# Batch 1's expert product in pairs of tiles, and its attention steps issued earlier

## Chip, cores, metric

One core of one Trainium2 chip. The metric is the time of one execution on the device in microseconds (us), median of several runs. TensorE's granted clock (PEclk in the profile, a share of its full speed) is near 1.0 in most runs, and where it is not, the text says so.

## The reference

Linear attention with an RMS norm per head, then layer norm, a two-layer expert with ReLU and a residual. Eight batches of 576 rows, 8 heads of 64.

```python
def _attn_ref(q, k, v, g_norm):          # q, k, v: (8, 8, 576, 64)
    kv = np.einsum('bhsd,bhse->bhde', k, v)
    out = np.einsum('bhsd,bhde->bhse', q, kv)
    rms = np.sqrt(np.mean(out * out, axis=-1, keepdims=True) + 1e-06)
    return out / rms * g_norm

def _moe_ref(x, g_ln, w_ch1, w_ch2):     # x: (8, 576, 512), w_ch1: (512, 2048)
    mu = np.mean(x, axis=-1, keepdims=True)
    var = np.mean((x - mu) ** 2, axis=-1, keepdims=True)
    xn = (x - mu) / np.sqrt(var + 1e-06) * g_ln
    return x + np.maximum(xn @ w_ch1, 0.0) @ w_ch2
```

## The kernel before

The expert's two products for each batch (`mm1`, `mm2`) fill TensorE from front to back. The attention of later batches is woven in between them by an agenda: the products are cut into slots of about 0.87 us, `tick()` starts a slot, and `at(slot, fn)` issues `fn` at its start, in front of that slot's matmuls. A fraction in a slot number only sets an order within the slot.

A batch has four tiles of 128 rows (and a rest). A turn is a transpose. One tile takes this path (shortened):

```python
    def plan_tile(s, make, turn_at, on_pe):
        def first():      # PE: attention product o; ACT: square; DVE: reduction
            t = make(); box.append(t)
            t.o(); t.sq(); t.red()
        def second():     # ACT: root; DVE: reciprocal, y, x, xc
            t = box[0]
            t.y(); t.x(); t.xc()
        def third():      # ACT: variance
            box[0].var()
        def fourth():     # PE: four transposes of xc; ACT: copy to xT_blk
            box[0].turn(on_pe)
        at(s, first); at(s + 2, second); at(s + 6, third); at(turn_at, fourth)
```

`turn` on TensorE uses `ps_m`, a pool of one bank, and `kv_of` (the k-v product of a batch) uses the same bank until ScalarE has cast it. A bank here is one buffer of such a pool. With one in the pool, the next user waits until the one before has been read out:

```python
    ps_m = ctx.enter_context(tc.psum_pool(name="ps_m", bufs=1))
    ps_out = ctx.enter_context(tc.psum_pool(name="ps_out", bufs=2))
# ... (cut)
                tp = ps_m.tile([128, nK, 128], bf16, tag="misc", name="tp")
                for kk in range(nK):
                    nc.tensor.transpose(tp[:, kk, :], self.xc_t[...], identity)
                nc.scalar.copy(dst, tp)
# ... (cut: kv_of)
        kv_ps = ps_m.tile([128, HP, D], f32, tag="misc", name="kv_ps")
        # 40 matmuls into kv_ps
        nc.scalar.copy(kvp[:D, :, :D], kv_ps[:D])
        nc.scalar.copy(kvp[D:, :, D:], kv_ps[D:])
```

Batch 1 turns its q on TensorE (`q_turns`). From batch 2 on, q is copied by VectorE and turned by a transposing DMA:

```python
    def turn_q_dma(b):
        q_p = kv_in.tile([128, JJ, H, D], bf16, tag="qp", bufs=2)
        nc.vector.tensor_copy(q_p.rearrange("p j h d -> p h j d"), q_in[b % NB])
        q_t = qt_pool.tile([128, JJ, HP, 128], bf16, tag="qt", name="qt")
        nc.sync.dma_start_transpose(q_t..., q_p...)
        qts[b] = q_t
```

The agenda that matters here, and the products. Batch 0's second product fills slots 16 to 31, batch 1's first one slots 32 to 47:

```python
    at(21, lambda: kv_of(1))
    q_turns(23, 1)
    for j, s, tn in ((0, 24, 30), (1, 27, 34), (2, 31, 38), (3, 35, 42)):
        plan_tile(s, lambda j=j: main_tile(1, j), tn, True)
    at(46, lambda: rstd_of(1))

    at(36, lambda: kv_of(2))
    at(36.5, lambda: turn_q_dma(2))
    for j, s, tn in ((0, 44, 50), (1, 48, 54), (2, 53, 61), (3, 58, 67)):
        plan_tile(s, lambda j=j: main_tile(2, j), tn, j > 1)
# ... (cut)
    for ts in range(4):
        mm1(1, ts, 1)          # one tile at a time: 128 columns
    mm2(1)
    mm1(2, 0, 2)               # batch 2: pairs, 256 columns
    mm1(2, 2, 2)
```

## Time and profile before

| | before |
|---|---|
| time, median of 3 runs | 291.68 us (291.61 to 291.71) |
| span of the profiled execution | 289.6 us |
| TensorE busy | 281.9 us, 97% |
| granted clock | 1.0 |

The page of the kernel before, its busy line and the shares of the chain of waits by engine (PE is TensorE, PEld its weight loads, DVE VectorE, ACT ScalarE, POOL GpSimd; L402 is line 402 of the kernel):

```profile
PE 281.9 (97%) x2312; PEld 158.6 (55%) x2312; DVE 151.0 (52%) x335; ACT 155.0 (54%) x339; POOL 41.0 (14%) x68
...
PE 93%; DMA 2%; ACT 1%; DVE 1%; POOL 1%; issue 1%; POOLq 0%
```

TensorE is the bound: the chain that ended last runs over it for 93% of the span.

The groups by line and shape, TensorE only, for the expert's first product (columns: line, engine, operation, operands, shape, count, then busy us and the mean ns of one):

```profile
L402 PE MATMUL p<-xT_blk,w_sb 128*128 128x128 bf16 x512 | 31.2, 219 | 0.2
L402 PE MATMUL p<-xT_blk,w_sb 128*128 128x256 bf16 x128 | 14.8, 273 | 0.0
```

The means (219 and 273 ns) are latencies of matmuls that overlap: the starts of the narrow ones are 55.9 ns apart. What one costs is read from starts in the timeline below.

The timeline of TensorE in the kernel before (start us, us, line, operation, operands, shape, count; a group's duration includes the modelled drain of its last matmul, so compare starts):

```profile
42.04 1.03 PE L418 MATMUL p<-w_sb,m 128*128 128x512 bf16 x4
43.13 0.38 PE L170 MATMUL tp<-identity,q_p 128*128 128x128 bf16 x4
...
57.05 0.39 PE L337 MATMUL tp<-identity,xc 128*128 128x128 bf16 x4
57.28 3.74 PE L402 MATMUL p<-xT_blk,w_sb 128*128 128x128 bf16 x64
60.85 0.39 PE L337 MATMUL tp<-identity,xc 128*128 128x128 bf16 x4
...
62.86 0.39 PE L260 MATMUL o_ps<-kv_pack,qt 128*128 128x128 bf16 x4
63.08 3.74 PE L402 MATMUL p<-xT_blk,w_sb 128*128 128x128 bf16 x64
66.66 0.39 PE L260 MATMUL o_ps<-kv_pack,qt 128*128 128x128 bf16 x4
```

Four matmuls of slot 23 start at 42.04 and take 0.86 (216 ns each: 20 of this shape, from 66.88, have the next product behind them at 71.20), so TensorE is free at 42.90; the q turn comes at 43.13, a gap of 0.23. The last three lines are batch 2's first attention product (`o_ps`, 62.86), 64 matmuls of 128 columns, and batch 2's next product: (66.66 - 63.08) / 64 = 55.9 ns each. From 57.05 to 66.66 there is no gap.

The timeline of VectorE in the kernel before, with batch 2's q copy (L201) and tile 3's y and xc:

```profile
56.48 0.82 DVE L201 COPY q_p<-q_in 128x2560 bf16<-128x2560 bf16 x1
...
58.19 0.69 DVE L292 TENSOR_TENSOR y<-o_ps,inv 128x512 f32<-128x512 f32 x1
...
59.84 0.75 DVE L321 SCALAR_TENSOR_TENSOR xc<-x_blk,st_blk,g_ln_sb 128x512 bf16<-128x512 f32 x1
```

The q copy runs ahead of tile 3's steps. It ends at 57.30, and the view of this DMA gives 5.0 us from issue (57.33) to landing, so q lies turned at 62.3. Batch 2's first product wants it at 62.86. There are 0.5 us to spare.

### The profile page before, as it was taken

The numbers are of one execution on the slowest core, as the hardware profiler recorded it, in microseconds if no ns is written. First come the engines' busy times: TensorE is split into PE (matmuls) and PEld (weight loads), VectorE is DVE, ScalarE is ACT, GpSimd is POOL, SyncE is SP. The second block draws the span as 40 slices with busy tenths as digits, with TensorE's granted clock in tenths as the row PEclk, the third lists the DMA queues.
The fourth block names the chain that finished last, engine by engine and source line by source line (L and its number), as shares of the span: only waits on it lengthen the run. The fifth ranks groups of instructions, "written<-read, shape, count | busy, mean of one in ns | idle before, by whom it ended". The sixth has DMA issues, their size and how long they took to land.

```text
span 289.6 us, 5791 instructions
## 1 busy us (share of the span) xinstructions
PE 281.9 (97%) x2312; PEld 158.6 (55%) x2312; DVE 151.0 (52%) x335; ACT 155.0 (54%) x339; POOL 41.0 (14%) x68
## 2 busy tenths in 40 slices
PE   7889999999999999999999999999999999999995
PEld 2579755996569644444444444444444444444444
DVE  5775028847997793765366925762578300220022
ACT  3467755885469832882189418920894076016500
POOL 8522520032032003200410023000000000000000
PEclk9999999999999999999999999999999999999999
DMA  7999999469999918995997179938202510131033
GB/s 215 203 206 203 201 202 218 109 99 188 155 177 160 151 40 158 205 167 102 148 208 103 42 146 194 178 75 164 54 18 53 112 36 0 38 81 28 0 74 73
DMA packets 64378, 36.10 MB, mean 125 GB/s; under 512 B 31836, under 2 KB 59356, under 8 KB 64352
## 3 DMA queue, kind: packets, MB, share of 16 engines
q0 software_dynamic: 28016, 17.76, 44.2%
q1 hardware_dynamic: 35824, 17.25, 30.5%
q10 hardware_dynamic: 512, 0.72, 0.7%
q8 instruction: 18, 0.29, 0.4%
q14 instruction: 8, 0.07, 0.1%
HBM read 36.71 MB, written 9.44 MB: 159 GB/s over the span
## 4 chain that ended last, share of the span: by engine, by line
PE 93%; DMA 2%; ACT 1%; DVE 1%; POOL 1%; issue 1%; POOLq 0%
PE p L418 43%; PE p L402 43%; PE o_ps L260 3%; DMA q_in<-in_q_dram 2%; PE kv_ps L235 2%; PE tp L183 1%; PE p L196 1%; PE tp L337 1%; ACT sq L266 0%; PE tp L170 0%; PE o_half L500 0%; POOL v_in L126 0%; ACT xT_blk L542 0%; ACT m L405 0%; DVE x_blk L278 0%
## 5 line engine op out<-in xcount | busy, mean ns | idle before, releaser
L402 PE MATMUL p<-xT_blk,w_sb 128*128 128x128 bf16 (+2 forms) x1024 | 131.8, 286 | 0.2
L418 PE MATMUL p<-w_sb,m 128*128 128x512 bf16 (+2 forms) x608 | 129.2, 368 | 0.0
L405 ACT ACTIVATE m<-p 128x512 bf16<-128x512 f32 x144 | 85.5, 596 | 43.3 <-PE p L402 41.1
L402 PEld LDWEIGHTS <-w_sb 128*128 128x128 bf16 x1024 | 78.5, 98 | 44.1 <-issue 0.6
L418 PEld LDWEIGHTS <-m 128*128 128x128 bf16 x608 | 56.8, 98 | 61.8
L423 DVE SCALAR_TENSOR_TENSOR o_sb<-p,rstd,x_blk 128x512 f32<-128x512 f32 (+2 forms) x38 | 27.4, 721 | 54.3 <-PE p L418 48.7
L266 ACT ACTIVATE sq<-o_ps 128x512 f32<-128x512 f32 x34 | 20.2, 595 | 41.5 <-PE o_ps L260 41.4
L287 DVE TENSOR_REDUCE ss<-sq 128x8 f32<-128x512 f32 x34 | 23.0, 678 | 11.2 <-ACT sq L266 11.2
L329 ACT ACTIVATE dev<-x_blk,st_blk 128x512 f32<-128x512 f32 x36 | 25.7, 714 | 4.6 <-DVE st_blk L315 4.4
L321 DVE SCALAR_TENSOR_TENSOR xc<-x_blk,st_blk,g_ln_sb 128x512 bf16<-128x512 f32 x34 | 25.6, 752 | 1.2
L292 DVE TENSOR_TENSOR y<-o_ps,inv 128x512 f32<-128x512 f32 x34 | 23.5, 692 | 3.0
L311 DVE SCALAR_TENSOR_TENSOR x_blk<-y,g_norm_sb 128x512 f32<-128x512 f32 x34 | 23.5, 692 | 1.2
L411 DVE RECIPROCAL rstd<-rstd 128x4 f32<-128x4 f32 x9 | 1.6, 174 | 35.3 <-ACT rstd L410 35.3
L304 DVE RECIPROCAL inv<-rms 128x8 f32<-128x8 f32 x36 | 7.2, 201 | 23.0 <-ACT rms L297 23.0
L98 POOL COPY gate<-qt 1x1 bf16<-1x1 bf16 x5 | 0.9, 178 | 114.1 <-DMA qt<-q_p 114.1
L297 ACT ACTIVATE rms<-ss,eps_sb 128x8 f32<-128x8 f32 x36 | 10.7, 297 | 9.5 <-DVE ss L287 8.8
L260 PEld LDWEIGHTS <-qt 128*128 128x128 bf16 (+1 forms) x152 | 9.9, 100 | 7.4 <-issue 1.7
L260 PE MATMUL o_ps<-kv_pack,qt 128*128 128x128 bf16 (+1 forms) x152 | 13.3, 220 | 0.2 <-DVE qt L191 0.2
L196 PE MATMUL p<-fill_sb 128*128 128x512 bf16 x28 | 8.1, 445 | 1.2 <-DVE eps_sb L137 1.2
L329 ACT ACTIVATION_READ_ACCUMULATOR dev<-x_blk,st_blk 128x1 f32 x36 | 6.9, 190 | 0.0
L235 PEld LDWEIGHTS <-k_in 128*64 128x64 bf16 x280 | 5.0, 112 | 2.6 <-issue 2.5
L238 ACT CAST kv_pack<-kv_ps 64x256 bf16<-64x256 f32 x7 | 2.6, 366 | 7.2 <-PE kv_ps L235 7.2
(79 smaller groups left out, 116.8 us busy)
## 6 DMA issues: line engine op xcount, KB each, us to landing
out_dram<-o_sb SPq DMA_DIRECT2D x70, 128.0 KB, 2.4
w_sb<-in_moe_w_ch_dram POOLq DMA_DIRECT2D x8, 512.0 KB, 13.8
k_in<-in_k_dram POOLq DMA_DIRECT2D x7, 320.0 KB, 5.8
v_in<-in_v_dram POOLq DMA_DIRECT2D x7, 320.0 KB, 9.4
q_in<-in_q_dram POOLq DMA_DIRECT2D x7, 320.0 KB, 12.7
q_in<-in_q_dram POOLq DMA_DIRECT2D x8, 256.0 KB, 12.7
k_in<-in_k_dram POOLq DMA_DIRECT2D x7, 256.0 KB, 7.3
v_in<-in_v_dram POOLq DMA_DIRECT2D x7, 256.0 KB, 11.3
```

The source lines that it names most:

```text
L196: nc.tensor.matmul(p1, lhsT=fill_sb[:, :128], rhs=fill_sb, start=True, stop=True)
L260: nc.tensor.matmul(flat[rows, hp * 128:(hp + 1) * 128], lhsT=lhsT_of(hp), rhs=kvp[:, hp, :], start=True, stop=True)
L266: nc.scalar.activation(self.sq_t, self.o_ps, func=AF.Square)
L287: nc.vector.tensor_reduce(self.ss, self.sq_t, axis=AX.X, op=ALU.add)
L292: nc.vector.tensor_mul(self.y_t, self.o_ps, self.inv().to_broadcast([128, H, D]))
L311: nc.vector.scalar_tensor_tensor(x_blk[:, ts].rearrange("p (h d) -> p h d", h=H), in0=self.y_t, scalar=1.0, in1=g_norm_sb.to_broadcast([12 ...
L321: nc.vector.scalar_tensor_tensor(self.xc_t, in0=x_blk[:, self.ts], scalar=st[:, 1, self.ts:self.ts + 1], in1=g_ln_sb, op0=ALU.add, op1=ALU ...
L329: nc.scalar.activation(dev, x_blk[:, ts], func=AF.Square, bias=st[:, 1, ts:ts + 1], accum_out=st[:, 2, ts:ts + 1])
L402: nc.tensor.matmul(p1[:, i, :], lhsT=w1_sb[:, kk, de * 128:(de + 1) * 128], rhs=blk[2][:, kk, sl], start=(kk == 0), stop=(kk == nK - 1))
L405: nc.scalar.activation(m1[:, de0:de0 + per, sl], p1, func=AF.Relu)
L418: nc.tensor.matmul(p2[:, c0:c1], lhsT=m1s[b][:, de, ts * 128:(ts + 1) * 128], rhs=w2_sb[:, de, c0:c1], start=(de == 0), stop=(de == nDe - 1))
L423: nc.vector.scalar_tensor_tensor(o_sb[:, c0:c1], in0=p2[:, c0:c1], scalar=rstds[b][:, ts:ts + 1], in1=blks[b][0][:, ts, c0:c1], op0=ALU.mu ...
```

## The change

Its intent: 256 columns for each matmul in place of 128 in batch 1's first product, so half as many matmuls and weight loads. A pair needs both its tiles before it starts, so all four tiles are issued one or two slots sooner, the q turns too, and the turn of every tile one to three. The core of the diff (context cut):

```diff
-    def plan_tile(s, make, turn_at, on_pe):
+    def plan_tile(s, make, turn_at, on_pe, behind=2):
...
-        at(s + 2, second)
+        at(s + behind, second)
...
             turn_q(b, 0, ps_out, "ops")
-            turn_q(b, 1, ps_m, "misc")
+            turn_q(b, 1, ps_out, "ops")
...
-    q_turns(23, 1)
-    for j, s, tn in ((0, 24, 30), (1, 27, 34), (2, 31, 38), (3, 35, 42)):
-        plan_tile(s, lambda j=j: main_tile(1, j), tn, True)
+    q_turns(21.5, 1)
+    for j, s, behind, tn in ((0, 23, 1, 28), (1, 25, 1, 31), (2, 29, 2, 37), (3, 33, 2, 39)):
+        plan_tile(s, lambda j=j: main_tile(1, j), tn, True, behind)
...
-    for ts in range(4):
-        mm1(1, ts, 1)
+    mm1(1, 0, 2)
+    mm1(1, 2, 2)
```

## The prediction

> **What bounds the kernel now.** TensorE. The page gives PE 281.9 us busy of a 289.6 us span, and the chain of waits gives PE 93%, at a granted clock of 1.0. From 37.7 us (agenda slot 21) to 66.9 us (end of batch 1's first product) the PE timeline has only about 0.4 us of gaps, most in slots 22 to 25: the chain shows the q turn at 43.13 us waiting for ACT's copy of the turn before, which stood behind a square.
>
> **Removed.** Batch 1's first product is 256 matmuls of 128 columns; it becomes 128 of 256. By starts in the PE timeline, 64 narrow ones take 3.57 us (55.8 ns each), 40 wide ones in batch 2 take 4.37 us (109.2 ns). So 14.29 us becomes 13.98: 0.31 us less. [...] The halved weight loads (98 ns each) are hidden: worth nothing. ACT's Relus keep count and size.
>
> **Moved.** q turns come 1.5 slots sooner (a slot is 0.86 to 0.89 us), tiles 1 to 2 slots. PE work stays, but its bank waits should go, as the copies no longer stand behind tile 0's square: up to 0.4 us gained. q should not be late: its copy on DVE ends at 38.25 us, the turns would start at 38.45.
>
> **New deadlines.** [...] A tile costs DVE about 3.15 us (reduction 0.6, then reciprocal to xc 2.55, start to start), and batch 0's outputs (0.65 each) stand between.
> - Tile 1's turn is now in slot 31, and slot 32 needs tiles 0 and 1. Adding durations: tile 0's xc ends near 45.8 us, in time for slot 28 (46.05). After tile 1's reduction, batch 0's first output and tile 1's steps, tile 1's xc ends near 49.6; PE reaches the turn at 49.1. Wait 0.5 us.
> - Tile 3's turn in slot 39 is needed in slot 40 (now 42 for 44). Its xc ends near 58.2, PE arrives near 58.05: wait 0.25 us. Its copy on ACT stands behind Relus and its own variance (0.71 us), lands near 60.0; PE is free at 59.45: 0.5 us more. In the kernel before, such a copy ends 1.7 us after the turn starts (57.05 to 58.8), covered by two slots; now one covers it.
>
> All of this is on the critical path, since PE is the bound and nothing later gives it back.
>
> **Sum.** -0.3 (wide) -0.4 (bank waits) +0.5 (tile 1) +0.25 +0.5 (tile 3) = +0.55; my waits may be too long, so I say **292.0 us**, 80% range **291.1 to 292.7**. With no new wait it would be 290.95. Faster by over 2%: 0.5%; within 2%: 99%; slower by over 2%: 0.5%.
>
> **What would show it.** By form: 256 first-product matmuls of 256 columns, 256 of 128. PE timeline: 109 ns between starts in batch 1; a gap near 49 to 50 us at tile 1's turn, released by DVE's xc; a gap near 59 to 60 us before the second pair, released by ACT's copy of xT; no wait at the q turns. Batch 2 unchanged.
>
> **What would make it wrong.** DVE or ACT through tiles 1 and 3 sooner than my sums: nearer 291. q landing later than the copy's start suggests: a wait at slot 21. Variance or Relus standing longer ahead of the copies: over 293. A bank of the p ring held by batch 0's late outputs, which I think are out near 50 us and needed near 52.

The sum: -0.3 -0.4 +0.5 +0.25 +0.5 comes to +0.55, and its -0.3 is the 0.31 us from the trace's own starts (55.8 and 109.2 ns). How one instruction stands behind another can be read in the trace of the kernel before: ScalarE's copy of the q turn of 41.82 starts at 42.50, behind the square begun at 42.01, and the next q turn comes at 43.13.

## The result and the profile after

293.53 us (293.29 to 293.94, 4 runs) against 291.69 (291.61 to 292.03, 4 runs). The ratio is 1.0062, 95% interval 1.0045 to 1.008: slower by 0.6%, and outside the predicted range. All ratios here are the mean time of one kernel's fast runs over that of the other's of the same rounds, so they are not quite the ratio of the medians quoted.

The page of the changed kernel, the same two lines:

```profile
PE 280.6 (96%) x2158; PEld 156.8 (54%) x2184; DVE 151.0 (52%) x335; ACT 155.8 (54%) x339; POOL 41.3 (14%) x68
...
PE 87%; DVE 5%; DMA 2%; ACT 2%; issue 1%; POOL 1%; DVEq 0%; POOLq 0%
```

TensorE is busy for 1.3 us less (some of that is records missing from the trace), the span is 1.6 us longer, and 5% of the chain of waits now runs over VectorE.

The groups of the changed kernel, in the same columns:

```profile
L402 PE MATMUL p<-xT_blk,w_sb 128*128 128x256 bf16 x256 | 29.9, 273 | 0.8 <-ACT xT_blk L339 0.8
L402 PE MATMUL p<-xT_blk,w_sb 128*128 128x128 bf16 x256 | 15.8, 219 | 0.2
```

The shapes changed as meant: 256 fewer of 128 columns, 128 more of 256 (batch 1's).

The timeline of TensorE in the changed kernel (in brackets: idle time before it, and who ended it). A few matmul records are missing here and there, so counts of 3 or 7 can stand for 4 or 8:

```profile
47.53 1.89 PE L418 MATMUL p<-w_sb,m 128*128 128x512 bf16 x8
49.84 0.40 PE L337 MATMUL tp<-identity,xc 128*128 128x128 bf16 x4 [0.42 <-DVE xc L321]
...
55.51 1.05 PE L402 MATMUL p<-xT_blk,w_sb 128*128 128x256 bf16 x8
57.00 0.38 PE L337 MATMUL tp<-identity,xc 128*128 128x128 bf16 x4 [0.45 <-ACT kv_pack L239]
57.22 1.91 PE L402 MATMUL p<-xT_blk,w_sb 128*128 128x256 bf16 x16
58.97 0.39 PE L337 MATMUL tp<-identity,xc 128*128 128x128 bf16 x4
59.19 1.04 PE L402 MATMUL p<-xT_blk,w_sb 128*128 128x256 bf16 x8
60.99 3.65 PE L402 MATMUL p<-xT_blk,w_sb 128*128 128x256 bf16 x32 [0.76 <-ACT xT_blk L339]
64.48 0.39 PE L260 MATMUL o_ps<-kv_pack,qt 128*128 128x128 bf16 x4
```

Reading it in starts: eight matmuls from 47.53 (216 ns each) end at 49.26, and tile 1's turn comes at 49.84 (0.58 us late). Eight wide ones from 55.51 (109 ns each) end at 56.38, tile 2's turn comes at 57.00 (0.62 late). Tile 3's turn at 58.97 is on time. Eight wide ones from 59.19 end at 60.06, and the second pair starts at 60.99 (0.93 late). That is 2.13 us of waiting. (The brackets, and the lists of waits below, count from the modelled end of the last matmul, so each wait is some 0.17 us shorter there.) Batch 2's first product, the last line, starts at 64.48.

ScalarE's timeline in the changed kernel, for the second and third of these waits:

```profile
55.53 0.30 ACT L297 ACTIVATE rms<-ss,eps_sb 128x8 f32<-128x8 f32 x1 [0.25 <-DVE ss L287]
55.74 0.58 ACT L405 ACTIVATE m<-p 128x512 bf16<-128x512 f32 x1
56.22 0.35 ACT L238 CAST kv_pack<-kv_ps 64x256 bf16<-64x256 f32 x1
56.59 0.37 ACT L239 CAST kv_pack<-kv_ps 64x256 bf16<-64x256 f32 x1
...
59.17 0.60 ACT L405 ACTIVATE m<-p 128x512 bf16<-128x512 f32 x1 [0.28 <-PE p L402]
59.66 0.71 ACT L329 ACTIVATE dev<-x_blk,st_blk 128x512 f32<-128x512 f32 x1
...
60.37 0.57 ACT L339 COPY xT_blk<-tp 128x512 bf16<-128x512 bf16 x1
```

ScalarE runs these in the order of issue. The root of tile 3 (L297) waits at 55.53 for VectorE's reduction, a Relu and the two casts of batch 2's kv come behind it, and the bank is free only at 56.96: that is what tile 2's turn waits for. Later the copy of tile 3's turn (L339) starts at 60.37, behind a Relu and the variance (L329).

VectorE's timeline in the changed kernel:

```profile
54.82 0.68 DVE L287 TENSOR_REDUCE ss<-sq 128x8 f32<-128x512 f32 x1
...
57.83 0.75 DVE L321 SCALAR_TENSOR_TENSOR xc<-x_blk,st_blk,g_ln_sb 128x512 bf16<-128x512 f32 x1
58.49 0.82 DVE L201 COPY q_p<-q_in 128x2560 bf16<-128x2560 bf16 x1
```

Tile 3's second part moved from slot 37 to 35 and batch 2's q copy stayed in slot 36.5, so their order is now reversed: y and xc come first, and the copy ends at 59.31, not 57.30. Its DMA lands 5.1 us after issue (59.34), between 64.4 and 64.5: GpSimd's copy that waits for this DMA alone (line 98, in GpSimd's timeline) starts at 64.48. Batch 2's first product starts at 64.48 too. No view of this kernel names the DMA as what the product waited for, because TensorE's own three waits brought it there at the same moment, by coincidence.

The start of every execution varies by some tenths, in some runs by 1.5 us (see below), so the traces are compared by an interval: from the start of batch 1's kv product to the start of batch 2's first attention product. It is 62.86 - 37.78 = 25.08 us before and 64.48 - 37.75 = 26.73 after, 1.65 longer. That is the loss.

### The profile page after: what moved, and what is told of

The parts are those of the page before. It is cut to its first block, busy times and chain, and to the rows that moved or that the text cites. A ratio compares the mean times of both kernels' runs of the same rounds, so it can differ in the third digit from the quotient of the medians.

```text
span 291.2 us, 5506 instructions
## 1 busy us (share of the span) xinstructions
PE 280.6 (96%) x2158; PEld 156.8 (54%) x2184; DVE 151.0 (52%) x335; ACT 155.8 (54%) x339; POOL 41.3 (14%) x68
## 4 chain that ended last, share of the span: by engine, by line
PE 87%; DVE 5%; DMA 2%; ACT 2%; issue 1%; POOL 1%; DVEq 0%; POOLq 0%
PE p L402 40%; PE p L418 40%; PE o_ps L260 3%; DMA q_in<-in_q_dram 2%; PE kv_ps L235 2%; DVE o_sb L423 1%; DVE ss L287 1%; DVE xc L321 1%; DVE x_blk L311 1%; DVE y L292 1%; PE tp L183 1%; ACT m L405 1%; PE p L196 1%; PE tp L337 0%; PE tp L170 0%
## 5 line engine op out<-in xcount | busy, mean ns | idle before, releaser
L402 PE MATMUL p<-xT_blk,w_sb 128*128 128x512 bf16 (+2 forms) x889 | 131.1, 302 | 1.4 <-ACT xT_blk L339 0.8
L418 PE MATMUL p<-w_sb,m 128*128 128x512 bf16 (+2 forms) x590 | 126.6, 368 | 1.5 <-issue 0.8
L402 PEld LDWEIGHTS <-w_sb 128*128 128x128 bf16 x896 | 76.1, 98 | 46.3 <-issue 1.6
L329 ACT ACTIVATE dev<-x_blk,st_blk 128x512 f32<-128x512 f32 x36 | 25.7, 715 | 5.1 <-DVE st_blk L315 4.9
L297 ACT ACTIVATE rms<-ss,eps_sb 128x8 f32<-128x8 f32 x36 | 10.7, 297 | 10.3 <-DVE ss L287 9.6
L329 ACT ACTIVATION_READ_ACCUMULATOR dev<-x_blk,st_blk 128x1 f32 x36 | 6.8, 190 | 0.0
```

What stands on the lines that cost most here:

```text
L329: nc.scalar.activation(dev, x_blk[:, ts], func=AF.Square, bias=st[:, 1, ts:ts + 1], accum_out=st[:, 2, ts:ts + 1])
L402: nc.tensor.matmul(p1[:, i, :], lhsT=w1_sb[:, kk, de * 128:(de + 1) * 128], rhs=blk[2][:, kk, sl], start=(kk == 0), stop=(kk == nK - 1))
L418: nc.tensor.matmul(p2[:, c0:c1], lhsT=m1s[b][:, de, ts * 128:(ts + 1) * 128], rhs=w2_sb[:, de, c0:c1], start=(de == 0), stop=(de == nDe - 1))
```

## The experiments

All times are medians, all ratios are against the kernel before in the same rounds. Every kernel gave correct results. The state counted as fast includes runs in which the clock was below 1.0 for a part of the time; where it matters they are named. It also includes single executions that are over 1 us longer at a clock of 1.0 (293.05 of before, 294.86 of e1_narrow), which nothing here explains.

| run | what it is | median us | ratio (95% interval) | interval in the trace, us |
|---|---|---|---|---|
| before | | 291.69 | | 25.08 |
| after | the change | 293.53 | 1.0062 (1.0045 to 1.0080) | 26.73 |
| e1_narrow | change, first product narrow | 293.35 | 1.0058 (1.0037 to 1.0078) | 26.63 |
| e2_bank | change, tile 2's turn in another bank | 293.80 | 1.0067 (1.0050 to 1.0083) | 26.80 |
| e3_var | change, tile 3's variance later | 293.47 | 1.0056 (1.0040 to 1.0072) | 27.09 |
| e4_bank_var | both | 293.55 | 1.0060 (1.0044 to 1.0077) | 26.87 |
| f1_qfirst | change, q copy first | 293.29 | 1.0051 (1.0037 to 1.0064) | 26.73 |
| f2_q_bank_var | all three | 292.32 | 1.0017 (1.0002 to 1.0032) | 25.75 |
| f3_soon | and tiles 0, 1 a slot sooner | 291.79 | 1.0008 (0.9988 to 1.0029) | 25.04 |
| f5_soon_late | f3 with the q copy late | 292.94 | 1.0035 (1.0022 to 1.0049) | 25.84 |
| g1_best | f3 without its last small waits | 291.26 | 0.9995 (0.9979 to 1.0012) | 24.65 |
| g2_best_narrow | g1 with the first product narrow | 291.29 | 0.9989 (0.9976 to 1.0002) | 24.85 |
| b1_late | before with the q copy late | 298.38 (298.07 without the run of 1671) | 1.0201 (1.0167 to 1.0235) | none usable |
| b2_late | the same again | 298.27 | 1.0227 (1.0206 to 1.0248) | 29.63 |

### Theory A first: only TensorE's waits for tiles

Theory A, formed from the trace: the loss is the three waits. Its rival, theory B: the wide form itself is slow here.

**e1_narrow**

```diff
-    mm1(1, 0, 2)
-    mm1(1, 2, 2)
+    for ts in range(4):
+        mm1(1, ts, 1)
```

> The changed kernel with batch 1's first product back in single tiles of 128 columns, all else as changed. Theory A (the loss is waits of TensorE for tiles that are needed sooner than VectorE and ScalarE give them): tile 3's columns are needed only in slot 44, so the 0.9 us wait for its copy goes; the wide product's 0.3 us gain is lost; the waits at the turns of tile 1 (0.5 us) and tile 2 (0.6 us) stay. Sum: 0.5 to 0.7 us faster than the changed kernel (about 292.8), still about 1 us slower than before. Theory B (the wide matmuls themselves are slower here than in batch 2): back to the time of before, 291.7, or below.

Measured 293.35, only 0.2 below the changed kernel. The third wait did go, but neither theory's number came: the trace shows a wait that neither had, 0.52 us at 64.32 for batch 2's transposed q. So this run doesn't settle theory B; g1 against g2 does, below.

**e2_bank**: a bank of the two-buffer pool for tile 2's turn.

```diff
-                tp = ps_m.tile([128, nK, 128], bf16, tag="misc", name="tp")
+                tp = (pool or ps_m).tile([128, nK, 128], bf16, tag=tag, name="tp")
...
+                  (ps_out, "ops") if j == 2 else (None, "misc")
```

> The changed kernel, with tile 2's turn (slot 37) written to a bank of the two-buffer pool in place of the single bank that batch 2's kv product holds until ScalarE has copied it. Theory A1 (the wait of 0.6 us at that turn is for the bank, which the prediction missed): the wait goes; then tile 3's turn meets xc, which VectorE ends near 58.6 us (wait 0.25 us), and the second pair starts near 60.3 in place of 61.0: 0.6 to 0.7 us faster than the changed kernel (about 292.8). Rival A2 (the wait is for tile 2's own xc, or ScalarE is the bound whatever the bank): no change, within 0.2 us.

Measured 293.80, no gain. The bank wait at tile 2's turn is gone (turn at 56.40, the second pair at 60.39 in place of 60.99, as A1 said), so the wait was for the bank. The 0.6 us did not reach the end. The list of who waited for whom, TensorE, 33 to 70 us, of e2_bank (total us, times, longest):

```profile
PE o_ps L260 <- DMA qt<-q_p: 0.5, 1, 0.5
```

**e3_var**

```diff
-        at(s + 6, third)
+        at(s + 6 if var_at is None else var_at, third)     # 42 for tile 3
```

> The changed kernel, with tile 3's variance on ScalarE issued in slot 42 in place of slot 39, so behind the copy of tile 3's turn. Theory A (the 0.9 us wait before the second pair is for that copy, 0.7 us of it because the variance stands ahead of it): the second pair starts 0.7 us sooner, 0.6 to 0.7 us faster than the changed kernel (about 292.8). Rival (the copy is late because tile 3 comes late from VectorE): no change.

Measured 293.47, no gain. The wait before the second pair shrinks to some 0.2 us (its 40 matmuls take 4.75 us, in e4_bank_var 4.53), and 0.7 us stand before batch 2's product instead. Its interval is the longest of the four in part because batch 1's q turns began later in the profiled execution: the first starts 0.92 us after the kv product (38.80 against 37.88), in the changed kernel 0.75.

**e4_bank_var**: both edits.

> Both: tile 2's turn in another bank and tile 3's variance behind the copy. Theory A with VectorE's chain under it: the two gains nearly add, but tile 3's turn then waits for xc (58.6 us), so 1.2 to 1.3 us faster than the changed kernel, about 292.2. Rival (one of the two hides the other): no more than 0.8 us faster.

Measured 293.55, no gain. The expected 1.2 us have moved as a whole into one new wait. The waits of TensorE in e4_bank_var, same columns:

```profile
PE o_ps L260 <- DMA qt<-q_p: 1.2, 1, 1.2
PE tp L337 <- DVE xc L321: 0.4, 1, 0.4
```

All four runs ended at the same place, near 293.5, however much TensorE's waits were cut. That is the mark of a second limit that ends at the same time. **Theory C**: batch 2's q copy on VectorE, which the change put behind tile 3's steps, and the DMA behind it. It gives batch 2's first product an earliest start near 64.4 us.

### Tests of theory C

**b1_late and b2_late**: the late copy alone, in the kernel before, with nothing else of the change.

```diff
-    at(36.5, lambda: turn_q_dma(2))
+    at(37.5, lambda: turn_q_dma(2))
```

> The kernel BEFORE, with one thing moved: VectorE's copy of batch 2's q (which feeds the transposing DMA) is issued in slot 37.5 in place of 36.5, so behind tile 3's y, x and xc. That is the order which the changed kernel has. Theory C (new: the changed kernel's time is set by this copy, since batch 2's first attention product waits for a DMA that lands 5.0 us after the copy): the copy ends near 61.3 us in place of 57.3, the DMA lands near 66.3, the product that stood at 62.9 waits until then: about 3.4 us slower than before, 295.1. Theory A (the loss is TensorE's waits for tiles alone, the copy's place is of no account): within 0.3 us of before.

Measured 298.38, with a wide spread: one execution of 1671 us, in which the profile fell and in which the matmul records are four times as long (line 402's mean is 1122 ns, before 286; a disturbance that no other run showed and that stays unexplained), and five from 295.65 to 298.99. The one of these at a granted clock of 1.0 took 295.65, close to the 295.1 expected; those at 0.988 took 298.1 to 299.0. So it was run again for a trace.

> The same kernel as b1_late (before, with the q copy of batch 2 behind tile 3's steps), again, since the profile of that one fell in an execution of 1671 us at a far slower TensorE, and its other five had granted clocks of 0.988 to 1.0. Theory C: the trace shows the copy ending near 61.3 us, the landing near 66.3 and batch 2's first attention product waiting about 3.4 us for it; time 295.2 at a granted clock of 1.0, and more (up to 299) where the clock falls[...]. Theory A: no wait there.

Measured 298.27 (297.47 to 299.35), all four runs at a clock of 0.988 to 0.994. The wait of TensorE in b2_late:

```profile
PE o_ps L260 <- DMA qt<-q_p: 4.4, 1, 4.4
```

Theory C's wait is there, and larger than expected (4.39 against 3.4 us; this DMA took 6.1 us to its use, not 5.0). The stretches of b2_late about that wait (us, then busy time of each engine, the granted clock PEclk, DMA share, GB/s):

```profile
core 0: us, PE busy (x) PEld busy (x) DVE busy (x) ACT busy (x) POOL busy (x), PEclk, DMA share, GB/s
64.00:68.80 4.80, 0.50 (x9) 0.33 (x6) 0.00 (x0) 0.99 (x2) 0.00 (x0) 1.00 1.09 140
68.80:70.00 1.20, 1.10 (x11) 1.11 (x12) 0.00 (x0) 0.40 (x1) 0.79 (x2) 0.50 0.00 0
70.00:72.00 2.00, 2.00 (x22) 2.00 (x20) 0.69 (x1) 0.80 (x2) 2.00 (x4) 0.50 0.58 47
```

After the wait the clock is at 0.50 for over three us (68.80 to 72.00; 0.90 in the next us), which costs some 1.5 us more (the next 64 matmuls take 4.96 us in place of 3.58, the product before them 0.41 in place of 0.22). In this execution 4.39 us of idle TensorE were followed by the half clock; that the one brought the other is not shown. If it did, the wait was paid for twice here. b1_late's run of 295.65 had a mean clock of 1.0 (its wait was not traced). The rest of b2_late's excess is at its start: it reached the kv product 1.5 us later than before (39.26 against 37.78).

So the place of one 0.82 us copy is worth several us in a kernel where nothing else was touched. This says that the order is a limit of its own.

**f1_qfirst**: the order of before, in the changed kernel.

```diff
-    at(36.5, lambda: turn_q_dma(2))
+    at(34.5, lambda: turn_q_dma(2))
```

> The changed kernel, with batch 2's q copy issued in slot 34.5, ahead of tile 3's y, x and xc (the order of before). Theory C with A: the DMA lands near 61.3 us, so it holds nobody, but the three waits of TensorE (turn of tile 1, turn of tile 2, copy of tile 3) stay and put batch 2's product at 64.5 to 65 us all the same: 0 to 0.3 us slower than the changed kernel, 293.5 to 293.8. Theory C alone (the copy is the whole loss): about 1.6 us faster, 291.9.

Measured 293.29, and the same interval as the changed kernel to 0.01 us. Undoing the copy's order alone gives at most 0.2 us, as C with A said. The copy ends at 56.52, but its DMA took 6.7 us here and landed at 63.2, not at the expected 61.3; that was still 1.5 us ahead of the product. The waits of TensorE in f1_qfirst:

```profile
PE p L402 <- ACT xT_blk L339: 0.8, 1, 0.8
PE tp L337 <- ACT kv_pack L239: 0.4, 1, 0.4
PE tp L337 <- DVE xc L321: 0.4, 1, 0.4
```

No DMA among them; the three of the changed kernel are back.

**f2_q_bank_var**: the q copy first, the other bank, the later variance.

> All three together: the q copy ahead of tile 3, tile 2's turn in the other bank, tile 3's variance behind the copy of its turn. The same bank and variance edits without the q copy gained nothing. Theory C with A (two limits at the same time, about 64.4 us: either alone gains nothing): now the second pair starts near 60.1 us and batch 2's product near 63.6, with only the wait at tile 1's turn (0.5 us) and one at tile 3's (0.6 us) left: 0.8 to 0.9 us faster than the changed kernel, 292.6. Rival: no gain again, which would mean a third limit.

Measured 292.32, 1.2 us faster than the changed kernel (expected 0.8 to 0.9). The q copy alone gave at most 0.2 us and the other two alone nothing. All that is left in the list of waits, in f2_q_bank_var:

```profile
PE tp L337 <- DVE xc L321: 0.8, 2, 0.4
```

**f3_soon**: tiles 0 and 1 one slot sooner.

```diff
-    for j, s, behind, tn in ((0, 23, 1, 28), (1, 25, 1, 31), (2, 29, 2, 37), (3, 33, 2, 39)):
+    for j, s, behind, tn in ((0, 22, 1, 28), (1, 24, 2, 31), (2, 29, 2, 37), (3, 33, 2, 39)):
```

> As the one before, and tiles 0 and 1 start one slot sooner (22 and 24, tile 1's second part behind batch 0's first output). VectorE's chain then starts about 1 us sooner. Expected: no wait at tile 1's turn, 0.1 to 0.3 us at tile 3's, batch 2's product near 62.4 us, against 62.9 before: 2.0 us faster than the changed kernel and 0.3 to 0.5 us faster than before, 291.2 to 291.4. If the wide product is worth nothing, no faster than 291.6.

Measured 291.79, ratio 1.0008: the loss is gone, but the expected gain over before did not come. Four runs took 291.55 to 291.98 and two, at a clock of 0.994, took 292.9 and 293.0. Its timeline still has about 0.5 us of small gaps: 0.2 before tile 0's product, 0.1 at the fourth q turn and 0.2 before the second pair. My claim of only 0.1 to 0.3 us left was too small.

**f5_soon_late**: f3 with the q copy back in slot 36.5.

> f3_soon (which shows no wait of TensorE over 0.2 us) with the q copy of batch 2 put back to slot 36.5, behind tile 3's y, x and xc, as in the changed kernel. Theory C with A (the late copy is a limit of its own): tile 3's steps end about 0.7 us sooner than in f3_soon, the copy ends near 58.1 us, the DMA lands 5.1 to 5.3 us later, 63.3, and batch 2's first attention product, which TensorE reaches near 62.7, waits 0.5 to 0.8 us: 0.5 to 0.8 us slower than f3_soon, 292.2 to 292.5. Rival (the copy's place costs only together with the other waits): the same as f3_soon.

Measured 292.94, 1.15 above f3's median (from other rounds; by the two ratios to before it is 0.27%, 0.8 us), and 0.80 by the interval. The wait, in f5_soon_late:

```profile
PE o_ps L260 <- DMA qt<-q_p: 0.6, 1, 0.6
```

With TensorE's other waits gone, the late copy costs 0.8 us by itself. It is a limit of its own in the changed schedule too.

### What the wide form is worth

**g1_best**: f3, with batch 1's kv cast by VectorE, and the copy of tile 3's turn on VectorE.

```diff
-        nc.scalar.copy(kvp[:D, :, :D], kv_ps[:D])
-        nc.scalar.copy(kvp[D:, :, D:], kv_ps[D:])
+        copy = nc.vector.tensor_copy if b == 1 else nc.scalar.copy
+        copy(kvp[:D, :, :D], kv_ps[:D])
+        copy(kvp[D:, :, D:], kv_ps[D:])
...
-                nc.scalar.copy(dst, tp)
+                copy(dst, tp)                 # nc.vector.tensor_copy for tile 3
...
-        at(s, start)
+        at(s - 1, start)                      # the q copy, ahead of the casts
+        at(s, turns)
```

> f3_soon with the two small waits that its trace still shows taken away: the casts of batch 1's kv go to VectorE (behind the q copy, which gets its own slot), so that ScalarE copies the first q turn sooner (0.2 us at tile 0's product), and the copy of tile 3's turn goes to VectorE too (0.2 us before the second pair). Theory: no wait over 0.1 us left between 38 and 67 us, 0.3 to 0.4 us faster than f3_soon: 291.3 to 291.4, faster than both kernels. Rival (some other limit holds the time at 291.7): no change.

Median 291.26. Four runs at a clock of 0.998 to 1.0 took 291.01 to 291.35; the other two, at 0.994, took 292.44 and 292.47, so the ratio's interval includes 1 and no gain over before is shown by times. (The four all lie below the lowest of before's eleven runs of these rounds, 291.56; but that picks runs after the fact.) The trace (one of the slow-clock ones) has lost its 1.5 us before 37 us: kv starts at 39.23, and the granted clock is 0.88 from 10 to 20 us and 0.97 from 20 to 37. After that its interval, 24.65, is 0.43 shorter than before's.

**g2_best_narrow**: the same with narrow matmuls.

> g1_best with batch 1's first product in single tiles of 128 columns. With no waits left the wide product alone is measured[...], so 0.3 us slower than g1_best. Rival (halved weight loads matter as well, 98 ns each): more than 1 us slower. Rival (the wide form is worth nothing): the same.

Where the 0.3 us comes from, the starts in the trace of before give: 2 x 55.8 - 109.2 = 2.4 ns for each of 128 matmuls, 0.31 us.

Median 291.29 (291.18 to 291.74), and no run at a low clock. The two timelines of TensorE, g1_best first (its lines are numbered one higher):

```profile
39.23 0.82 PE L235 MATMUL kv_ps<-v_in,k_in 128*64 128x64 bf16 x40
...
63.88 0.39 PE L261 MATMUL o_ps<-kv_pack,qt 128*128 128x128 bf16 x4
64.11 3.66 PE L403 MATMUL p<-xT_blk,w_sb 128*128 128x256 bf16 x32
67.60 0.39 PE L261 MATMUL o_ps<-kv_pack,qt 128*128 128x128 bf16 x4
```

```profile
37.70 0.82 PE L235 MATMUL kv_ps<-v_in,k_in 128*64 128x64 bf16 x40
...
62.55 0.39 PE L261 MATMUL o_ps<-kv_pack,qt 128*128 128x128 bf16 x4
...
66.35 0.39 PE L261 MATMUL o_ps<-kv_pack,qt 128*128 128x128 bf16 x4
```

From kv to batch 2's second product (`o_ps` in the last line) it is 67.60 - 39.23 = 28.37 us wide and 66.35 - 37.70 = 28.65 narrow: 0.28 us for 128 matmuls saved, 2.2 ns each. The times cannot show so little (four good runs of g1, mean 291.15; five of g2, mean 291.36). The gain that the change was made for is 0.28 us, about 0.1%, and g2 has most of what g1 has without it. So the wide form is not slow here, which answers theory B.

## Why the prediction was wrong, point by point

- **The bound, the columns, the weight loads: right.** Wide matmuls gave 0.28 us in g1 against g2, predicted 0.31, and the 128 weight loads saved (98 ns each, one for each matmul, while the narrow matmuls start every 55.9 ns) show no gain beyond that.
- **"Bank waits should go ... up to 0.4 us gained": right in kind, too large.** Before, the third and fourth q turns were late by 0.23 and 0.10 us. After, only the fourth is, by 0.10. The term is 0.23 us.
- **Tile 1's turn, "Wait 0.5 us": right**, 0.58 measured.
- **Tile 2's turn: missed.** I had not listed it. Its bank was held by batch 2's kv product, one slot ahead in place of two, and the casts stood on ScalarE behind a root that waited for VectorE. 0.62 us, and e2 showed that it was the bank.
- **Tile 3's turn, "wait 0.25 us": absent**, because TensorE came later through the wait above. In e2, where that wait is gone, it is there: TensorE is free at 58.37 and the turn starts at 58.64.
- **Tile 3's copy, "0.5 us more": 0.93**, since the variance and a Relu ahead of it started later than I thought. The prediction had named this as what would bring the time over 293; alone it adds 0.43.
- **The failed step: the list under "New deadlines", and "Batch 2 unchanged".** The prediction took the waits of tiles 1 and 3 for all that could come late to TensorE. Two things were not on the list. The first is tile 2's turn, which waited 0.62 us for its bank. With it the five measured terms (-0.28 -0.23 +0.58 +0.62 +0.93 = +1.62, predicted +0.55) add up to the trace's 1.65; of the 1.07 us by which the sum was short, 0.62 are this wait and 0.43 tile 3's copy. The second is a limit at the same place: I checked the q load of batch 1, and not the q of batch 2, whose copy the change overtook on VectorE, so that it landed at 64.4 to 64.5 us in place of 62.3. Had my waits been as small as predicted (+0.55), batch 2's product would still have waited for its DMA until about 64.4, against 62.86 before: about 1.5 us slower. That is an estimate from the copy's end (59.31) and the 5.1 us to landing; e4 shows nearly that case, with 1.2 us less waiting by TensorE and no time won.

Why is VectorE's order so tight? The chain of waits of the changed kernel runs over it from 43.3 to 55.5 us without a gap worth naming: tiles 0 to 2 at some 3.15 us each, with batch 0's outputs (0.66 each) between, and then tile 3's reduction. Who comes first there decides who is late. The traces show it for one copy: issued behind tile 3's steps in b2_late, it started at 62.0 us in place of 56.5 (1.5 of that is the late start of that run).

What stays open: why some executions lose clock between 10 and 37 us, as the traces of g1_best and b2_late show (0.88 from 10 to 20 us, 0.97 from 20 to 37; before's run of 293.10 has a mean clock of 0.994, which fits such a stretch, but no trace), and the single execution of 1671 us.

## What to carry to other kernels

When work is moved up on an engine that runs it in the order of issue, as VectorE did here (the overtaken copy started at 58.49 us in place of 56.48), look at what it overtakes, and follow that to its consumer, across a DMA too: the slack of 0.5 us behind the 5.0 us transfer was not seen in the list of waits before, because nobody waited yet. When taking a wait away gains nothing, look for a second limit that ends at the same time, and take both away. And count first what a change can win at best: here 0.28 us, against 0.5 us of slack that it needed.

## What the traces show besides

- With a weight load for each matmul (2312 of each in before), the stream runs at 55.9 ns a matmul with 128 columns ((66.66 - 63.08) / 64 in before), at 109.1 ns with 256 ((67.60 - 64.11) / 32 in g1_best) and at 216 ns with 512 ((71.20 - 66.88) / 20 in before).
- The transposing DMA of batch 2's q, 128x2560 elements of 2 bytes (0.66 MB), lands 5.0 to 5.3 us after issue in seven of the twelve traces that were read for it, 6.0 in b2_late, and 6.6 to 6.7 in f1_qfirst, f2_q_bank_var, f3_soon and g1_best; why is not shown. That is 98 to 131 GB/s from issue to landing; in e4_bank_var the engines moved 288 to 292 GB/s from 62.25 to 63.75 us, near its end (64.6).
- In g1_best and b2_late the clock is 0.88 from 10 to 20 us and 0.97 from 20 to 37, though TensorE was busy for 8.77 of those 10 us and 16.94 of those 17; the kernel before was busy for 8.61 and 16.94 us in the same places and kept a clock of 1.0. In g1_best this goes with a mean clock of 0.994 and a kv product that starts 1.5 us late.
